# Reading modulation and weight blocks in 128-row transfers, and running V's first products chunk by chunk

## The chip, the cores and the metric

The kernel runs on one core of a Trainium2 chip. The metric is the device time of one execution in microseconds; of several runs the median is given.

## The reference

One transformer block over 2048 tokens of width D = 448 with 16 heads of 28, all in fp32. A condition vector `c` (448 values) gives six rows of modulation:

```python
mod = (silu(c) @ w_mod).reshape(1, 6, 1, 448)      # w_mod: 448 x 2688
sa, ca, ga, sb, cb, gb = (mod[:, i] for i in range(6))
h = layernorm(x) * (1 + ca) + sa
x = x + ga * mha(h, wqkv, wo)                      # softmax attention, wqkv: 448 x 1344
h = layernorm(x) * (1 + cb) + sb
x = x + gb * gmlp(h, w_in, w_sp, b_sp, w_out)      # GELU, spatial mix over 2048 tokens
```

The change concerns the start: `sa` and `ca`, the first layer norm, and V's products of the first 512 tokens.

## The kernel before

**Staging.** The program is one long order written by hand: each engine runs its instructions in the order of the text, and waits come only from data and buffers. Tokens are taken in four groups of 512 (`g`), each of four tiles of 128 (`t`, `kt`). The width of 448 is cut into four chunks `c` of 128, 128, 128 and 64 rows; the chunks are worked in the order 0, 2, 1, 3. Products keep fp32 accuracy by two parts: `hi` is the value rounded for the fast fp32 matmul, `lo` the remainder. The operand `hT[g]` has seven blocks: 0 to 2 the `hi` and 3 to 5 the `lo` of chunks 0 to 2, block 6 `hi` and `lo` of the 64-row chunk one above the other. A weight has eight: 0 to 2, 3 to 5 likewise, 6 the `hi` of the 64-row block on both halves of the partitions, 7 its `lo` with zeros. A product is eleven steps `(a, b)` (a block of `hT`, a block of the weight) that add up in one bank: `STEPS`.

**The 64-row block (the z block).** `load_z` (L86 to L88) reads the last 64 rows of a weight twice, into partitions 0 to 63 and 64 to 127, with two DMAs. It is used for V's weight and for parts `a` (512 columns) and `b` (384 columns) of the q/k weight (`load_w`, L194), and later for `wo` (`wo_load`), and the two halves of `w_in` (`win_first`, tile `wraw`; `win_load`, tile `raw_in`).

**Modulation.** `w_mod` comes as four blocks of 112 rows for each of three pairs (`load_mod`, L176). For pair 0 (`sa`, `ca`) all four blocks are scaled by `silu(c)` and added up over rows on ScalarE and VectorE (L380, L241, `mod_last` L407); `mod_dot` (L420) sums over partitions with a product by ones, so that each chunk's columns lie on partitions; `mod_cols` (L427, L429) puts them into `cols["ca"]` and `cols["sa"]`. Pairs 1 and 2 are added up later in the same way (`mod_acc`).

**First group.** `load_x(0)` is issued from the ScalarE and SyncE queues. `pe_fill` (L230) runs products on TensorE whose result is not used, between the real ones. `ln_stat`, `ln_rs`, `ln_norm` (L279 to L298) normalise x, `xn` gets a copy of its last 64 columns on ScalarE, and `tp_first` (L371) transposes it into four banks `tps[c]`. `h_hi(c)` (L441, ScalarE) scales and rounds a chunk into `hT[0]`; `h_full(c)` (L436, VectorE) gives it unrounded, `h_lo(c)` (helper L84) the remainder. `wv_hi` (L352, L354) and `wv_lo` (L84) split V's weight. `v_step(j, kts)` (L477) runs step `j` for the given tiles.

**After V.** ScalarE runs `qk_hi(0)`, `qk_hi(2)`, `qk_hi(3)` (L512, the `hi` of part `a`), `v_copy` of tile 0 (L309), `qk_hi(1)`, and `v_copy` of the others; VectorE runs the statistics of group 1, `qk_lo` for blocks 0, 2, 1, 3, and `ln_norm(1)`. TensorE goes on with `qk_unit((0, 3), 0, order=HI_FIRST)` (L323), two banks at a time: steps (0,0), (2,2), (3,0), (5,2), (1,1), (4,1), (6,6), and then the `lo` steps. Step (1,1) is the first that reads what `qk_hi(1)` writes, so it is the ninth product. Then come the transposes of group 1 (L117), and so on through four groups, the attention, the output product and the MLP.

**DMA.** SyncE issues nearly all transfers, in the order of the text; an issue waits until the buffer is free and an earlier transfer on the same semaphore has landed. In the attention `n_bcast` (L707) reads a row per 512 queries with `[:, None, :].broadcast_to([4, 32, 512])` into 128 partitions.

Of the kernel before, what the change touches and what calls it, by code (L numbers as in the profile page):

```python
# [33 lines left out]
def tile_adaln_mha_gmlp(ctx, tc, x, wqkv, wo, w_in, w_spT, b_sp, w_out, cT, w_mod, out):  # L34
# [21 lines left out]
    silu = const.tile([112, 4], F32, name="silu")  # L56
# [6 lines left out]
    heapF = dpool.tile([128, 4 * 896], F32R, name="heapF", tag="heapF")  # L63
# [17 lines left out]
    wqk = Halves(4, hview(heapD[2], 0, 4, 896), hview(heapF, 0, 4, 896))  # L81

# [3 lines left out]
    def load_z(eng, dst, src):  # L86
        eng.dma_start(dst[0:64], src)
        eng.dma_start(dst[64:128], src)  # L88
# [71 lines left out]
    ones_r = e2.tile([112, 128], F32R, name="ones_r")  # L160
# [6 lines left out]
    def bank(name):  # L167
        k = mode[0](name) if mode[0] else banks[0]
        banks.remove(k)
        banks.append(k)  # L170
        return ring.tile([128, 512], F32, name=name, tag=f"b{k}")

    def load_mod(pair, eng):
        for k in range(4):
            wms[pair, k] = e1.tile([112, 2, D], F32, name="wm", tag=("wm", "wm", "raw")[pair], bufs=4)
            eng.dma_start(wms[pair, k], w_mod[:, pair, k])  # L176

    def load_x(g, eng):
        xg = e1.tile([128, 4, D], F32, name="xg")
        for t0, t1 in ((0, 1), (1, 2), (2, 4)) if g == 0 else ((0, 4),):  # L180
            (act if t1 - t0 == 1 else eng).dma_start(xg[:, t0:t1, :], x[g, :, t0:t1])
        for t in range(4):
            xts[4 * g + t] = xg[:, t, :]
# [23 lines left out]
    cc_t = e1.tile([112, 4], F32, name="cc_t", bufs=1)  # L207
# [7 lines left out]
    pool.memset(wqk[64:128, 7, 0:896].bitcast(F32), 0.0)  # L215
# [3 lines left out]
    ec = e1.tile([112, 4], F32, name="ec", bufs=1)  # L219
    act.activation(ec, cc_t, AF.Exp, scale=-1.0)  # L220
    dve.tensor_scalar(out=ec, in0=ec, scalar1=1.0, scalar2=None, op0=ALU.add)
    dve.reciprocal(ec, ec)
    dve.tensor_tensor(out=silu, in0=cc_t, in1=ec, op=ALU.mult)

    pcs = {c: bank("pc") for c in (0, 2)}
# [8 lines left out]
    def mod_acc(pair, k):  # L234
        if k == 0:
            accs[pair] = e2.tile([112, 2, D], F32, name="acc")
        wm, acc = wms.pop((pair, k)), accs[pair]
        if k == 0:
            dve.tensor_scalar(out=acc, in0=wm, scalar1=silu[:, 0:1], scalar2=None, op0=ALU.mult)
        else:  # L240
            dve.scalar_tensor_tensor(out=acc, in0=wm, scalar=silu[:, k : k + 1], in1=acc, op0=ALU.mult, op1=ALU.add)  # L241

    def mod_split(pair, eng, pool_l, tag_l, bufs_l):

        acc = accs.pop(pair)
        accs[pair] = []
        for part in range(2):
            h = stage.tile([128, 512], F32R, name="acc_h", tag="qf")[0:112, :D]
            l = pool_l.tile([112, D], F32R, name="acc_l", tag=tag_l, bufs=bufs_l)
# [32 lines left out]
    def ln_rs(g, a, e):  # L282
        mv, rs = mv1[g]
        rstd_of(mv[:, a:e, 1], rs[:, a:e], e - a)
# [15 lines left out]

    def v_mm(kt):
# [47 lines left out]
    def wv_hi(i):  # L349
        h = wv[:, i if i < 3 else 6, :]  # L350
        if i == 2:
            pool.tensor_copy(h, raws["v", i])  # L352
        else:
            act.activation(h, raws["v", i], AF.Copy)  # L354
# [8 lines left out]


    tps, fs = {}, {}
# [3 lines left out]
    def tp_first(t):  # L369
        for c in range(4):  # L370
            pe.transpose(tps[c][:, t * 128 : (t + 1) * 128], xn1[0][t][:, c * 128 : (c + 1) * 128], ident)  # L371

    x0, x3 = xts[0], xts[3]
    pe_fill(14, x0)
    ln_stat(0, (0, 1))
    ln_rs(0, 0, 2)
    ln_stat(0, (2, 3))
    ln_rs(0, 2, 4)
    accs[0] = e2.tile([112, 2, D], F32, name="acc")
    act.activation(accs[0], wms.pop((0, 0)), AF.Copy, scale=silu[:, 0:1])  # L380
    ln_norm(0, (0, 1))
    mod_acc(0, 1)
    tp_first(0)
    tp_first(1)
    ln_norm(0, (2, 3))
    mod_acc(0, 2)
    pe_fill(5, x3)
    tp_first(2)
    tp_first(3)
    pe_fill(2, x3)  # L390

    acc0 = [stage.tile([128, 512], F32, name="acc0", tag="qh")[0:112] for _ in range(2)]
    wm3 = wms.pop((0, 3))

    def mod_last(c):
        for part in (1, 0):
            if c < 3:
                o = acc0[part][:, c * 128 : (c + 1) * 128]  # L400
                a, w = (v[:, part, c * 128 : (c + 1) * 128] for v in (accs[0], wm3))
            else:
                o = acc0[part][:, 384:512].rearrange("p (r n) -> p r n", n=64)
                a, w = (
                    v[:, part, 384:D].rearrange("p (r n) -> p r n", r=1).broadcast_to([112, 2, 64]) for v in (accs[0], wm3)
                )
            dve.scalar_tensor_tensor(out=o, in0=w, scalar=silu[:, 3:4], in1=a, op0=ALU.mult, op1=ALU.add)  # L407

    def mod_dot(c, which):
        if c == 1:  # L410
            pcs[c] = ps_o.tile([128, 512], F32, name="pc", tag="o")
        if c == 3:
            pcs[c] = pcs[1][:, 2:4]
        for i, part in enumerate((1, 0)):
            cs = slice(c * 128, (c + 1) * 128)
            if which == "C":
                o, lhs, rhs = 2 + i, wm3[:, part, cs], silu[:, 3:4]
            else:
                o, lhs, rhs = i, (accs[0][:, part] if which == "A" else acc0[part])[:, cs], ones[:112, 0:1]
            pe.matmul(pcs[c][:, o : o + 1], lhs, rhs, start=True, stop=True)  # L420

    def mod_cols(c):
        for i, (nm, plus1) in enumerate((("ca", 1.0), ("sa", 0.0))):
            o = cols[nm][:, c : c + 1]
            if c == 0:
                a, b = pcs[c][:, i : i + 1], pcs[c][:, 2 + i : 3 + i]
                dve.tensor_scalar(out=o, in0=a, scalar1=b, scalar2=plus1, op0=ALU.add, op1=ALU.add)  # L427
            else:
                dve.tensor_scalar(out=o, in0=pcs[c][:, i : i + 1], scalar1=plus1, scalar2=None, op0=ALU.add)  # L429

    def h_full(c):
        if c < 2:
            fs[c] = e1.tile([128, 512], F32, name="hfull")
        else:
            fs[c] = stage.tile([128, 512], F32, name="hfull", tag="qf")
        dve.tensor_scalar(  # L436
            out=fs[c], in0=tps[c], scalar1=cols["ca"][:, c : c + 1], scalar2=cols["sa"][:, c : c + 1], op0=ALU.mult, op1=ALU.add
        )
# [12 lines left out]
    for i in (0, 2, 1, 3):  # L451
        load_w("a", i, sp)
    wv_hi(0)
    wv_hi(2)
    mod_dot(0, "C")
    mod_dot(0, "A")
    mod_last(2)
    pe_fill(2, x3)
    mod_dot(2, "all")
    pe_fill(4, x3)  # L460
    mod_cols(0)
    h_hi(0)
    mod_cols(2)
    h_hi(2)
    mod_last(1)
    mod_last(3)
    wv_hi(1)
    wv_lo(0, dve)


    order = [STEPS[j] for j in (0, 1, 6, 2, 3, 4, 7, 5, 8, 9, 10)]
    pvs = [(kt, bank("pv") if kt < 3 else None) for kt in range(4)]
# [9 lines left out]
    mod_dot(1, "all")  # L482
    mod_cols(1)
    h_hi(1)
    wv_hi(3)
    v_step(1, (0, 1, 2))
    mod_dot(3, "all")
    wv_lo(2, dve)
    h_full(0)
    mod_cols(3)  # L490
    h_hi(3)
    v_step(2, (0, 1, 2))
    pvs[3] = (3, ps_o.tile([128, 512], F32, name="pv", tag="o"))
    for j in range(3):
        v_step(j, (3,))
    h_lo(0, pool)
    h_full(2)
    h_full(1)
    wv_lo(1, dve)
    h_lo(2, dve)  # L500
    h_lo(1, dve)
    h_full(3)
    h_lo(3, dve)
    wv_lo(3, dve)
    load_x(2, sp)
    for i in (0, 2, 1, 3):
        load_w("b", i, sp)
    for j in range(3, NST):
        v_step(j, range(4))

# [976 lines left out]
```

## Time and profile before

| | us |
|---|---|
| median of 3 runs | 1397.21 |
| lowest, highest | 1396.95, 1399.44 |
| span of the profiled execution, first to last instruction | 1394.0 |
| TensorE busy in it | 1386.8 |
| VectorE, ScalarE, GpSimd busy | 1027.5, 776.5, 285.5 |

For the profiled execution the profile has the span alone, without what lies around it; the median of the runs lies 3.2 us above that span. Lines of the profile give a start and a duration in us, the engine (PE is TensorE's products, PEld its weight loads, DVE VectorE, ACT ScalarE, POOL GpSimd, SPq SyncE's issue of DMAs), the line of the kernel, the tiles written and read, the shape, and in brackets the idle time before, with what ended it. A product in plain fp32 appears as two passes.

### The profile page before, as it was taken

The page shows a single profiled execution, that of the slowest core. Times are in us where ns is not written, and L with a number is a line of the kernel's source. Part 1 is how long each engine was busy: PE and PEld are TensorE (multiplying, and loading weights), DVE is VectorE, ACT ScalarE, POOL GpSimd, SP SyncE. Part 2 cuts the span into 40 slices and gives each one's busy share as a digit, 9 for nine tenths or more (in the row PEclk, how much of TensorE's full clock was granted, in tenths as well). Part 3 has the DMA queues.
Part 4 walks back from the last instruction along what each step waited for, and adds up shares of the span by engine and source line. Part 5 has one row for each costly group of instructions (what it writes and reads, how often), then busy time and mean ns, then how long its engine had stood idle before and what let it go on. Part 6 is the DMA issues. An engine that isn't in the chain of part 4 may idle for free.

```text
span 1394.0 us, 20327 instructions
## 1 busy us (share of the span) xinstructions
PE 1386.8 (99%) x7180; PEld 988.9 (71%) x7180; DVE 1027.5 (74%) x1741; ACT 776.5 (56%) x1490; POOL 285.5 (20%) x306
## 2 busy tenths in 40 slices
PE   8999999999999999999999999999999999999999
PEld 8888655555555555555555555988998888888888
DVE  7798888888888888888888851750366655668574
ACT  4623677777766667777777779363234544434211
POOL 2234213221224143323200021000142330000000
PEclk9999999999999999999999999999999999999999
DMA  8564644565465556554323002434103333445453
GB/s 265 150 178 177 196 109 151 172 177 154 149 178 167 162 159 189 165 161 150 111 68 76 21 18 73 161 123 140 46 4 110 113 109 112 143 137 163 142 174 110
DMA packets 99377, 187.01 MB, mean 134 GB/s; under 512 B 17736, under 2 KB 29130, under 8 KB 96730
## 3 DMA queue, kind: packets, MB, share of 16 engines
q1 hardware_dynamic: 96558, 181.42, 42.6%
q10 hardware_dynamic: 2718, 4.30, 0.9%
q8 instruction: 56, 0.92, 0.3%
q14 instruction: 45, 0.37, 0.1%
HBM read 130.42 MB, written 50.46 MB: 130 GB/s over the span
## 4 chain that ended last, share of the span: by engine, by line
PE 99%; DMA 0%; DVE 0%; ACT 0%; ACTq 0%; issue 0%
PE st_ps L666 19%; PE o_ps L681 17%; PE mt L634 17%; PE acc L1250 7%; PE acc L1252 7%; PE acc L1251 7%; PE z_ps L1176 5%; PE pq L323 5%; PE z_ps L1062 5%; PE wo_ps L928 3%; PE pv L305 2%; PE y_ps L1357 2%; PE y_ps L1358 2%; PE y_ps L1356 2%; PE tp L117 1%; PE pv L477 1%
## 5 line engine op out<-in xcount | busy, mean ns | idle before, releaser
L639 DVE TENSOR_REDUCE pm<-mt 128x1 f32<-128x512 f32 x1024 | 631.1, 682 | 85.6 <-PE mt L634 85.5
L670 ACT ACTIVATE P<-st_ps 128x512 f32<-128x512 f32 x1024 | 514.5, 628 | 200.8 <-PE st_ps L666 200.7
L666 PE MATMUL st_ps<-qst,kst 128*128 128x512 f32 x1024 | 404.1, 406 | 0.0
L634 PE MATMUL mt<-kst,qst 128*128 128x512 f32 x1024 | 401.7, 392 | 0.0
L666 PEld LDWEIGHTS st_ps<-qst,kst 128*128 128x128 f32 x1024 | 191.2, 187 | 141.2 <-issue 93.1
L681 PE MATMUL o_ps<-P,V 128*32 128x512 f32 x2048 | 247.1, 598 | 0.0
L634 PEld LDWEIGHTS mt<-kst,qst 128*128 128x128 f32 x1024 | 192.4, 188 | 31.8
L791 POOL TENSOR_TENSOR ws_raw<-ws_raw 128x512 f32<-128x512 f32 x80 | 103.2, 1290 | 293.8 <-DMA ws_raw<-in_w_spT_dram 290.9
L1138 ACT ACTIVATE wsp_h<-raw_sp 128x512 fp32r<-128x512 f32 x112 | 70.0, 630 | 153.6 <-PE acc L1252 102.9
L84 DVE TENSOR_TENSOR wsp_l<-raw_sp,wsp_h 128x512 fp32r<-128x512 f32 x112 | 80.7, 730 | 83.1 <-ACT wsp_h L1138 82.3
L681 PEld LDWEIGHTS o_ps<-P,V 128*32 128x32 f32 x2048 | 54.7, 109 | 122.0 <-issue 114.0
L1250 PE MATMUL acc<-wsp_h,heapA 128*128 128x512 f32 x224 | 87.3, 390 | 0.0
L1251 PE MATMUL acc<-wsp_l,heapA 128*128 128x512 f32 x224 | 87.2, 389 | 0.0
L1252 PE MATMUL acc<-wsp_h,heapA 128*128 128x512 f32 x224 | 87.2, 389 | 0.0
L1251 PE MATMUL acc<-wsp_l,heapB 128*128 128x512 f32 x174 | 67.7, 389 | 0.0
L1252 PE MATMUL acc<-wsp_h,heapB 128*128 128x512 f32 x174 | 67.7, 389 | 0.0
L1250 PE MATMUL acc<-wsp_h,heapB 128*128 128x512 f32 x174 | 67.7, 389 | 0.0
L323 PE MATMUL pq<-heapD,heapD 128*128 128x512 f32 x196 | 61.8, 390 | 0.0
L1180 DVE BATCH_NORM_STATS2 stz<-z 128x6 f32<-128x448 f32 x32 | 19.9, 625 | 50.4 <-ACT z L1179 30.1
L1250 PEld LDWEIGHTS acc<-wsp_h,heapA 128*128 128x128 f32 x224 | 42.0, 188 | 8.9 <-DVE cD L1256 0.3
L1252 PEld LDWEIGHTS acc<-wsp_h,heapA 128*128 128x128 f32 x224 | 42.0, 188 | 8.8
L1251 PEld LDWEIGHTS acc<-wsp_l,heapA 128*128 128x128 f32 x224 | 42.0, 188 | 8.6
(222 smaller groups left out, 1597.0 us busy)
## 6 DMA issues: line engine op xcount, KB each, us to landing
ws_raw<-in_w_spT_dram SPq DMA_DIRECT2D x160, 256.0 KB
ws_scr<-ws_raw SPq DMA_DIRECT2D x80, 256.0 KB
raw_sp<-ws_scr SPq DMA_DIRECT2D x80, 256.0 KB
kst<-qk_scr SPq DMA_DIRECT2D x45, 224.0 KB
qst<-qk_scr SPq DMA_DIRECT2D x45, 224.0 KB
raw_sp<-in_w_spT_dram SPq DMA_DIRECT2D x32, 256.0 KB
qk_scr<-qh SPq DMA_DIRECT2D x28, 256.0 KB
qk_scr<-ql SPq DMA_DIRECT2D x28, 256.0 KB
```

Of the source, the lines that this page charges most:

```text
L84: eng.tensor_tensor(out=dst, in0=a, in1=hi.bitcast(F32), op=ALU.subtract)
L323: pe.matmul(pq, wqk[:, b, m * 128 : (m + 1) * 128], hT[g][:, a, :], start=j == 0, stop=j == NST - 1)
L634: pe.matmul(mt, qst[h % 3][:, t * 128 : (t + 1) * 128], kst[h % 3][:, kb * 512 : (kb + 1) * 512], start=True, stop=True)
L639: dve.tensor_reduce(out=pms[h][:, t, kb : kb + 1], in_=mt, axis=AX.X, op=ALU.max)
L666: pe.matmul(st, kst[h % 3][:, kt * 128 : (kt + 1) * 128], qst[h % 3][:, qb * 512 : (qb + 1) * 512], start=True, stop=True)
L670: act.activation(p, st, AF.Exp, scale=SCALE)
L681: pe.matmul(otile[h][32 * qb : 32 * qb + 32, :], V[:, kt, h, :], ptiles.pop((u, qb)), start=kt == 0, stop=kt == NT - 1)
L791: pool.tensor_tensor(out=a, in0=a, in1=b, op=SUMS[i // 16][2])
L1138: act.activation(hi, raw, AF.Copy)
L1250: pe.matmul(acc[i], zh, hi, start=st == 0, stop=False)
L1251: pe.matmul(acc[i], zh, lo, start=False, stop=False)
L1252: pe.matmul(acc[i], zl, hi, start=False, stop=st == 7)
```

## The change

- **w_mod, pair 0**: laid out by column chunk, each chunk one transfer of 128 rows (`load_mod0`): for a chunk of n columns, three row blocks of 128 for both parts, and the last 64 rows of the two parts one above the other. `silu` gets five columns to match. Pairs 1 and 2 are read by blocks of 128 rows, the last 64 rows of both parts in one block.
- **Order of the loads**: w_mod and V's weight alternate by chunk; x of the first group comes in four transfers; part `a` of the q/k weight is issued further down in the text, after V's last weight step.
- **z blocks**: `load_z` is one DMA with a source of `[2, 64, n]`, the 2 repeated.
- **Modulation**: chunk 0 goes straight through TensorE (`mod_direct`, eight products into one column each); the other chunks are scaled and added up by chunk (`acc_first` on ScalarE, `acc_rest` on VectorE), then `mod_dot` and `mod_cols`.
- **V**: the eleven steps are ordered by chunk, so that chunk 0's three steps run before chunk 2's data are made, and so on. `h_full` moves to ScalarE, `h_lo(0)` to VectorE, `wv_hi(2)` to ScalarE. The fills between the transposes and the dots go, 13 remain at the start.
- **Buffers**: pair 0 of w_mod lies in the buffer that later holds half of the q/k weight; the memset of its block 7 moves behind V.

```diff
     def load_z(eng, dst, src):
-        eng.dma_start(dst[0:64], src)
-        eng.dma_start(dst[64:128], src)
+        eng.dma_start(dst, src[None, :, :].broadcast_to([2, 64, src.shape[-1]]))
...
+    def load_mod0(c, eng):
+        n = 128 if c < 3 else 64
+        v = wm0[:, c * 896 : c * 896 + 7 * n]
+        eng.dma_start(v, w_mod0[c * 896 * 128 : (c * 896 + 7 * n) * 128].rearrange("(r n) -> r n", r=128))
+        wms[0, c] = v[:, 0 : 6 * n].rearrange("r (k p n) -> r k p n", k=3, p=2), v[:, 6 * n :]
...
-    load_mod(0, sp)
     for i in (0, 2, 1, 3):
+        load_mod0(i, sp)
         load_w("v", i, sp)
     load_x(1, sp)
...
+    def half_rows(wm, outs):
+        for part, o in enumerate(outs):
+            dve.scalar_tensor_tensor(out=o, in0=wm, scalar=silu[:, 3 + part : 4 + part], in1=o, op0=ALU.mult, op1=ALU.add)
...
+    def mod_direct(c):
+        wm, wh = wms.pop((0, c))
+        for i, part in enumerate((1, 0)):
+            for k in range(3):
+                pe.matmul(pc_of(c, i), wm[:, k, part, :], silu[:, k : k + 1], start=k == 0, stop=False)
+            pe.matmul(pc_of(c, i), wh, silu[:, 3 + part : 4 + part], start=False, stop=True)
+
+    def acc_first(c):
+        n = 128 if c < 3 else 64
+        o = acc0[c] = stage.tile([128, 512], F32, name="acc0", tag="qh")[:, 0 : 2 * n].rearrange("p (a n) -> p a n", n=n)
+        act.activation(o, wms[0, c][0][:, 0], AF.Copy, scale=silu[:, 0:1])
+
+    def acc_rest(c):
+        (wm, wh), o = wms.pop((0, c)), acc0[c]
+        for k in (1, 2):
+            dve.scalar_tensor_tensor(out=o, in0=wm[:, k], scalar=silu[:, k : k + 1], in1=o, op0=ALU.mult, op1=ALU.add)
+        half_rows(wh, [o[:, part] for part in range(2)])
...
+    x0 = xts[0]
+    pe_fill(13, x0)
+    ln_norm(0, (0, 1))
     wv_hi(0)
+    mod_direct(0)
+    for t in (0, 1):
+        for c in range(4):
+            tp_first(c, (t,))
+    acc_first(2)
+    ln_norm(0, (2, 3))
+    for c in (0, 2, 1, 3):
+        tp_first(c, (2, 3))
     mod_cols(0)
+    acc_rest(2)
     h_hi(0)
+    h_full(0)
     wv_lo(0, dve)
+    order = [(0, 0), (0, 3), (3, 0), (2, 2), (2, 5), (5, 2), (1, 1), (1, 4), (4, 1), (6, 6), (6, 7)]
...
     v_step(0, (0, 1, 2))
+    mod_dot(2)
+    mod_cols(2)
+    h_lo(0, dve)
+    acc_first(1)
+    wv_hi(2)
     v_step(1, (0, 1, 2))
+    v_step(2, (0, 1, 2))
+    h_hi(2)
+    h_full(2)
+    acc_rest(1)
     wv_lo(2, dve)
+    mode[0] = lambda name: tp0_bank
+    pvs.append((3, bank("pv")))
+    mode[0] = None
     for j in range(3):
         v_step(j, (3,))
+    v_step(3, range(4))
+    mod_dot(1)
+    mod_cols(1)
+    wv_hi(1)
+    h_hi(1)
     h_full(1)
+    acc_first(3)
+    h_lo(2, dve)
     wv_lo(1, dve)
+    v_step(4, range(4))
+    v_step(5, range(4))
     h_lo(1, dve)
+    acc_rest(3)
+    v_step(6, range(4))
+    mod_dot(3)
+    mod_cols(3)
+    wv_hi(3)
+    h_hi(3)
     h_full(3)
     h_lo(3, dve)
     wv_lo(3, dve)
+    for i in (0, 2, 1, 3):
+        load_w("a", i, sp)
     load_x(2, sp)
     for i in (0, 2, 1, 3):
         load_w("b", i, sp)
-    for j in range(3, NST):
+    for j in range(7, NST):
         v_step(j, range(4))
```

More of the change, by code (lines that the diff above doesn't have):

```diff
@@ L33, in tile_adaln_mha_gmlp @@
 @with_exitstack
[L34 removed]
+def tile_adaln_mha_gmlp(ctx, tc, x, wqkv, wo, w_in, w_spT, b_sp, w_out, cT, w_mod0, w_mod, out):
     nc = tc.nc
@@ L55, in tile_adaln_mha_gmlp @@
     dve.memset(mhalf, -0.5)
-    silu = const.tile([112, 4], F32, name="silu")
+    silu = const.tile([128, 5], F32, name="silu")
     cols = {}
@@ L214, in tile_adaln_mha_gmlp @@
     pool.memset(wv[64:128, 7, :].bitcast(F32), 0.0)
-    pool.memset(wqk[64:128, 7, 0:896].bitcast(F32), 0.0)
     pool.memset(V[:, :, :, DH:32], 1.0)
[L219 to L225, printed above, removed]
+    ec = e1.tile([128, 5], F32, name="ec", bufs=1)
     wu = bank("wu")
@@ L299, in ln_norm @@
             xn1.setdefault(g, []).append(xn)
+    ln_stat(0, (0, 1))
+    act.activation(ec, cc_t, AF.Exp, scale=-1.0)
+    dve.tensor_scalar(out=ec, in0=ec, scalar1=1.0, scalar2=None, op0=ALU.add)
+    dve.reciprocal(ec, ec)
+    dve.tensor_tensor(out=silu, in0=cc_t, in1=ec, op=ALU.mult)
+    ln_rs(0, 0, 2)
+    ln_stat(0, (2, 3))
+    ln_rs(0, 2, 4)
     def v_mm(kt):
@@ L361, in wv_lo, with tp_first @@
             sub(eng, wv[0:64, 7, :], raw[0:64], wv[0:64, 6, :])
-    tps, fs = {}, {}
+    tps, fs, acc0 = {}, {}, {}
+    tp0_bank = banks[0]
     for c in (0, 2, 1, 3):
         tps[c] = bank("tp")
-    def tp_first(t):
-        for c in range(4):
+    def tp_first(c, ts):
+        for t in ts:
             pe.transpose(tps[c][:, t * 128 : (t + 1) * 128], xn1[0][t][:, c * 128 : (c + 1) * 128], ident)
[L373 to L413, printed above, removed]
-        for i, part in enumerate((1, 0)):
[L415 to L420, printed above, removed]
+    def pc_of(c, i):
+        return wu[:, 256 + 2 * c + i : 257 + 2 * c + i]
@@ new lines, in acc_rest, with mod_dot @@
+    def acc_rest(c):
[3 more added lines that the diff above has]
+        half_rows(wh, [o[:, part] for part in range(2)])
+    def mod_dot(c):
+        for i, part in enumerate((1, 0)):
+            a = acc0[c][:, part]
+            for r0, r1 in ((0, 128),) if c < 3 else ((0, 64), (64, 128)):
+                pe.matmul(pc_of(c, i)[r0:r1], a, ones[:, 0:1], start=True, stop=True)
@@ L449, in h_lo @@
             sub(eng, hT[0][64:128, 6, :], fs[3][64:128], hT[0][64:128, 6, :])
-    for i in (0, 2, 1, 3):
-        load_w("a", i, sp)
+    x0 = xts[0]
+    pe_fill(13, x0)
+    ln_norm(0, (0, 1))
     wv_hi(0)
[L454 to L460, printed above, removed]
+    mod_direct(0)
[6 more added lines that the diff above has]
+        tp_first(c, (2, 3))
     mod_cols(0)
+    acc_rest(2)
     h_hi(0)
[L463 to L467, printed above, removed]
+    h_full(0)
     wv_lo(0, dve)
-    order = [STEPS[j] for j in (0, 1, 6, 2, 3, 4, 7, 5, 8, 9, 10)]
-    pvs = [(kt, bank("pv") if kt < 3 else None) for kt in range(4)]
+    order = [(0, 0), (0, 3), (3, 0), (2, 2), (2, 5), (5, 2), (1, 1), (1, 4), (4, 1), (6, 6), (6, 7)]
+    pvs = [(kt, bank("pv")) for kt in range(2)]
+    pvs.append((2, ps_o.tile([128, 512], F32, name="pv", tag="o")))
     def v_step(j, kts):
@@ L507, in tile_adaln_mha_gmlp @@
         load_w("b", i, sp)
-    for j in range(3, NST):
+    for j in range(7, NST):
         v_step(j, range(4))
+    heapF = dpool.tile([128, 4 * 896], F32R, name="heapF", tag="heapF")
+    wqk = Halves(4, hview(heapD[2], 0, 4, 896), hview(heapF, 0, 4, 896))
+    pool.memset(wqk[64:128, 7, 0:896].bitcast(F32), 0.0)
     def qk_hi(i):
@@ L1471 @@
         "w_out": inputs["B_w_out"],
-        "cT": inputs["c"].reshape(4, 112).T,
-        "w_mod": _np.asarray(inputs["w_mod"]).reshape(4, 112, 3, 2, 448).transpose(1, 2, 0, 3, 4),
+        "cT": cT,
+        "w_mod0": _np.concatenate([rows(0, c, min(c + 128, 448)) for c in (0, 128, 256, 384)]),
+        "w_mod": _np.concatenate([_np.concatenate([blocks(i, k) for k in range(4)]) for i in (1, 2)]),
     }
```

69 lines of the change are left out of this document (30 added, 39 removed).

## The prediction

> **What bounds the kernel now.** First the page: its span, and its chain that ended last.
>
> ```profile
> span 1394.0 us, 20327 instructions
> PE 99%; DMA 0%; DVE 0%; ACT 0%; ACTq 0%; issue 0%
> ```
>
> TensorE sets the end almost everywhere, so a microsecond by which its unbroken stream starts sooner or later is a microsecond of the result. The change touches the first 25 us. So the second view is the chain of waits in order of time over the first stages (start, duration, what):
>
> ```profile
> 16.20 0.16 DVE col_sa L429
> 16.39 0.79 ACT heapD L441
> 17.22 8.02 PE pv L477 x38
> 25.24 5.02 PE pq L323 x22
> 30.25 1.75 PE tp L117 x16
> ```
>
> The last wait outside TensorE is the ScalarE step at 16.39 (`h_hi(1)`). From 17.22 on, V's remaining 38 products (0.211 each), the first q/k unit (22 products, 0.228 each) and the next transposes (0.109 each) follow without a gap. The reference point of the sum is the **ninth q/k product**, the first that needs `qk_hi(1)`: 25.24 + 8 x 0.228 = 27.07 us. Its shift in the changed kernel is the shift of the end.
>
> **Prices.** Timeline (start, duration, engine, line, tiles), with the waits in brackets:
>
> ```profile
> 3.61 5.06 PE L230 MATMUL wu<-ones,xg 128*128 128x128 f32 x28 [3.61 <-DMA xg<-in_x_dram]
> 12.30 0.51 PE L420 MATMUL pc<-silu,wm 112*128 112x1 f32 x4
> 14.90 0.85 PE L477 MATMUL pv<-wv,heapD 128*128 128x448 f32 x3
> 13.74 1.54 ACT L441 ACTIVATE heapD<-tp,col_sa,col_ca 128x512 fp32r<-128x512 f32 x2 [0.84 <-DVE col_sa L427]
> 14.32 1.13 DVE L407 SCALAR_TENSOR_TENSOR acc<-wm,silu,acc 112x128 f32<-112x128 f32 x4
> 19.62 1.29 DVE L84 TENSOR_TENSOR heapD<-hfull,heapD 128x512 fp32r<-128x512 f32 x2
> 18.51 1.15 ACT L512 ACTIVATE heapD<-raw 128x512 fp32r<-128x512 f32 x2
> 21.41 0.63 ACT L512 ACTIVATE heapF<-raw 128x512 fp32r<-128x512 f32 x1 [1.76 <-DMA raw<-in_wqkv_dram]
> 24.67 0.55 ACT L309 ACTIVATE V<-pv 128x448 f32<-128x448 f32 x1 [2.62 <-PE pv L477]
> 25.11 0.62 ACT L512 ACTIVATE heapD<-raw 128x512 fp32r<-128x512 f32 x1
> ```
>
> The reader should see the ScalarE order at the end: `qk_hi(0)`, `qk_hi(2)`, then `qk_hi(3)`, which waited until 21.41 for the z block of part a, then `v_copy(0)`, then `qk_hi(1)` at 25.11. Today that wait ends 3.3 us before `v_copy(0)` could start, so it costs nothing.
>
> Next the windows of the transfers (columns: stretch, length, busy of PE, PEld, DVE, ACT, POOL, clock, DMA share of 16 engines, GB/s), and the two ends of the one kind of transfer here that has a leading broadcast, `n_bcast` (source `[4, 32, 512]`, the 32 repeated, 256 KB):
>
> ```profile
> 2.00:4.00 2.00, 0.39 (x2) 0.42 (x3) 0.52 (x4) 1.15 (x2) 1.56 (x2) 1.00 0.94 324
> 4.00:6.00 2.00, 2.00 (x11) 2.00 (x11) 1.05 (x4) 0.00 (x0) 0.00 (x0) 1.00 1.07 354
> 6.00:12.00 6.00, 5.93 (x47) 5.55 (x47) 5.44 (x12) 1.85 (x5) 2.19 (x4) 1.00 1.03 288
> 16.00:18.00 2.00, 1.93 (x12) 1.71 (x13) 1.87 (x7) 1.41 (x3) 0.31 (x1) 1.00 1.03 385
> 213.40:214.60 1.20, 1.20 (x7) 0.98 (x6) 1.20 (x3) 1.20 (x4) 1.19 (x1) 1.00 0.25 99
> 210.79 0.58 SPq L707 DMA_DIRECT2D rb<-r_scr  x1
> 217.04 1.28 POOL L710 TENSOR_TENSOR osb<-osb,rb 128x512 f32<-128x512 f32 x1 [2.33 <-DMA rb<-r_scr]
> 838.07 0.59 SPq L707 DMA_DIRECT2D rb<-r_scr  x1
> 842.96 1.28 POOL L710 TENSOR_TENSOR osb<-osb,rb 128x512 f32<-128x512 f32 x1 [9.93 <-DMA rb<-r_scr]
> ```
>
> **Part 1, w_mod in 128 rows, by chunk.** The loads of 112 rows ran in 6 to 12 us at 288 GB/s; in 16 to 18, where whole 128-row blocks were on the way, 385. To the last w_mod chunk the changed queue carries x (0.92 MB), w_mod (1.61) and three V blocks (0.69): 3.21 MB. From 2.0 us, where the share jumps to 0.94, that ends at 10.3 at 385 GB/s and at 13.1 at 288. I take 10.6, near the 128-row rate, since all of these are now 128 rows. The first chunk is due when the fills end (8.2, below) and lies at 5.6 to 6.8 in the stream, so its landing has over 1 us of cover; the later chunks have more.
>
> **Part 2, V's products chunk by chunk.** The fills are 26 passes instead of 28. Two windows of the fill line (stretch, length, busy PE and PEld, clock, DMA share, GB/s) give their pitch:
>
> ```profile
> 3.60:7.00 3.40, 3.39 (x16) 3.40 (x17) 1.00 1.05 342
> 7.20:8.50 1.30, 1.30 (x13) 1.28 (x12) 1.00 1.01 276
> ```
>
> Sixteen passes took 3.4 us (0.21 each), then 0.11 each. So the fills end at 3.61 + 17 x 0.21 + 9 x 0.11 = 8.2. `mod_direct(0)` is 8 products of two passes; four passes took 0.51 alone, some 0.11 each in a row: 1.7, to 9.9. Then transposes: chunk 0 is whole after 10 of 16, with the drain at 11.2. `h_hi(0)` 0.79: 12.0. V's first product starts there, against 14.90 before, but the waits now lie inside V:
> - three products 0.63, `mod_dot(2)` and its two columns 0.7 (0.51 with the drain, 0.16 and a hand-over): 13.3. VectorE's `h_lo(0)` 0.65: 13.95. Ten products (steps 1 and 2 are partly there already, tile 3's three, and step 3) 2.1: 16.05.
> - `mod_dot(1)` and its columns 0.7: 16.75. `h_hi(1)`, `h_full(1)`, both now on ScalarE, 1.54: 18.3. VectorE: `h_lo(1)` 0.65, then `acc_rest(3)` (two of 128 elements at 0.28, two of half that, about 0.2): 1.0, to 19.95.
> - `mod_dot(3)`, four products of half width, and columns 0.85; `h_hi(3)` and `h_full(3)` 1.54; `h_lo(3)` 0.65: 23.0. The last eight products 1.7: **24.7**.
>
> TensorE's own work would fill only up to 22.6 (12.0, 44 products, 1.3 of dots); DVE and ACT hold it. With 0.1 more in each of a dozen hand-overs it is 26.0. V thus ends 0.5 us earlier (2.6 earlier to 0.8 later). The fills taken out between are worth nothing: TensorE waits there anyway. `h_lo(0)` and `wv_hi(2)` leave POOL, whose steps were not on the chain; the wqk memset now waits for w_mod's last reader (20 us), still before `qk_hi(3)`.
>
> **Part 3, z blocks in one transfer.** `load_z` becomes one DMA whose source is `[2, 64, n]` with the 2 repeated. No such transfer is in the trace; the nearest is `n_bcast`. While it ran alone (213.40 to 214.60) a quarter of the 16 engines was busy and moved 99 GB/s: four engines, one for each entry of the outermost dimension, 24.7 GB/s each. So I take two engines for the outermost 2. The price for one engine's 64 KB was, less the issue, 842.96 - 838.66 = 4.30 us in the quiet case, 217.04 - 211.37 = 5.67 beside other loads. 2.66 of it is the transfer at 24.7 GB/s, 1.64 lies around it; in the busy case the transfer took 4.03. For V's z block (112 KB an engine) that makes 4.7 to 7.1 us, for part a's (128 KB) 5.3 to 8.1, where sixteen engines need 0.6 and 0.7.
>
> The Trainium skill speaks against this form: "DMA: Bandwidth & Descriptors", section "Rules for kernel authors", says that an outermost dimension under 16, a leading zero-stride broadcast for one, confines the whole DMA to at most that many engines. The quarter in the trace agrees for 4; no run here shows 2 yet. By that rule the sum is the one that follows; with sixteen engines it would be that of the first rival.
>
> That both z blocks and the rest share the two engines in order of issue is my inference. Then they carry: the stream to 10.6; V's z, 6.6 (fourteen engines are busy with x(1) and part a, so near the slow end) to 17.2; their sixteenth of x(1) (57 KB) 2.35; of three blocks of a (49 KB) 2.0; a's z, 5.9 (the others have little left by then, so near the quick end) to 27.45; landing 0.8, half of the 1.64: **28.25**. Then `qk_hi(3)` 0.53, `v_copy(0)` 0.44, both by start-to-start in the rows above, `qk_hi(1)` 0.62, hand-overs 0.06: the ninth q/k product at 29.9 instead of 27.07, **+2.85 us**. TensorE has done its eight by 26.5 and waits. Behind `qk_hi(3)` on ScalarE stand the V copies and `xn`'s pads; behind `qk_hi(1)` VectorE's `qk_lo(1)`, `qk_lo(3)` and `ln_norm`, which shift with it and so give nothing back. V's own z block lands at 18.0 and is wanted by `wv_hi(3)` before `h_hi(3)` at 20.8: covered by 2 us.
>
> Bounds: with everything at the free rate a's z lands at 10.3 + 4.7 + 2.35 + 2.0 + 5.3 + 0.8 = 25.4, and the shift is 0.0; with the slow ends 13.1 + 7.1 + 2.35 + 2.0 + 8.1 + 0.8 = 33.4, +8.0.
>
> The part-a loads move down in the text, but on SP they still follow x(1) and no longer wait for w_mod's buffers. The three later z loads are hidden:
>
> ```profile
> 556.57 0.60 SPq L88 DMA_DIRECT2D wo_raw<-in_wo_dram  x1
> 562.56 1.16 POOL L750 TENSOR_TENSOR wo_raw<-wo_raw,bc_ga 128x448 f32<-128x448 f32 x1
> 783.35 0.59 SPq L88 DMA_DIRECT2D wraw<-in_w_in_dram  x1
> L1006 ACT ACTIVATE heapA<-wraw x4: 935/936/937, 866.0 to 868.5; 128x896 fp32r<-128x896 f32 x4
> 944.40 0.59 SPq L88 DMA_DIRECT2D raw_in<-in_w_in_dram  x1
> 959.24 0.94 ACT L95 ACTIVATE heapF<-raw_in 128x896 fp32r<-128x896 f32 x1
> ```
>
> (The fourth row is the line's summary: count, shortest, median and longest in ns, first and last start.) The first has 6 us, the second 80, the third 15 (224 KB an engine: 9.3 to 14.1). If the cover is gone, POOL or ACT starts a few us late, with TensorE banks in hand. The two halves of w_mod's last block in the later pairs cost VectorE a fraction of a us under TensorE's products.
>
> **The sum.** +2.85 on a span of 1394.0; the median of the runs shown, 1397.21, lies 3.2 above that span, and I add the shift to it: **1400.1**. The 0.2% that a measurement of this kernel can tell from no change is 2.8 us.
>
> **Rivals.**
> - *The broadcast is spread over sixteen engines, or the two blocks use different ones* (faster, no wait): a's z lands before 22, `qk_hi(3)` follows at once, and V's 0.5 us gain stands: 1396.7. It decides if a's z lands before 24.9. Against it speaks the quarter above. Chance 0.12.
> - *Two engines at the free rate*: shift 0.0, 1397.2. For it: 99 GB/s held on four engines; against it the 4.03 beside other loads. Chance 0.14.
> - *The stall cools TensorE*: it waits from 26.5 to 29.9, 3.4 us, and the fills show a slow first 3.4 us after idleness. If the pitch doubles again for as long, 3.4 us do the work of 1.7: +4.55, 1401.8. Against it: nothing in this trace shows a restart after a short wait. Chance 0.18. The skill's "TensorE: Matmul & The Clock Gate", Part 1, gives an idle window of about 3.4 us for this; the first fills agree with its busy window.
> - *DVE and ACT overlap better than I sum, and no z wait*: V ends at 22.6, 1394.6. Chance 0.03.
>
> **The numbers.** Forecast (two engines, contended) 0.53, over +1 to +6. Half of it and a bit (0.31) lies above 2.8 us, with the cooled case 0.49 slower. Faster by over 0.2% needs a little more than the last rival gives: 0.03. The rest, 0.48, is within. The range runs from the no-wait case, 1396.3, to 1403.3 (+6.1), the slow end of a's z leaving out its most extreme sum.
>
> **What would show it.** Right: `qk_hi(3)` (heapF from raw) starts near 28 with a long DMA wait; the DMA share falls to an eighth while a z block runs alone; V starts at about 12 and ends near 24.7 with gaps before `mod_dot(3)`; the ninth q/k product near 30. Wrong: a's z lands before 25, a gap over 3 us remains inside V, or SP's order puts the z blocks elsewhere.

## The result, and the profile after

| | before | after |
|---|---|---|
| median, us | 1397.14 (9 runs) | 1400.67 (9 runs) |
| lowest, highest | 1395.40, 1399.44 | 1399.50, 1402.07 |
| span of the profiled execution | 1394.0 | 1399.8 |

The ratio is 1.0029, with a 95% interval of 1.0019 to 1.0038: slower by 3.5 us. The forecast was 1400.1. The two profiled executions lie 5.8 us apart, since one is at the low end of its runs and the other in the upper half of its own. So steps are compared by place below, and kernels by medians.

The page of the changed kernel, its span and the engines' shares of the chain that ended last, reads nearly as before:

```profile
span 1399.8 us, 20294 instructions
PE 98%; DMA 1%; issue 0%; SPq 0%; ACT 0%; DVE 0%
```

One per cent more stands on transfers. Below, "the z wait" is the wait for the z block of part `a`: through `qk_hi(3)`, `v_copy(0)` and `qk_hi(1)` on ScalarE it holds TensorE's ninth q/k product. The chain of waits, over the stretch that the prediction showed (start, duration, what):

```profile
11.95 11.14 DMA raw<-in_wqkv_dram
23.09 1.05 ACT heapD L512 x2
24.14 3.94 issue
28.07 0.63 ACT heapF L512
28.70 0.43 ACT V L324
29.14 0.53 ACT heapD L512
29.71 5.08 PE pq L338 x14
34.79 1.75 PE tp L114 x16
```

The unbroken stream of TensorE now begins at the ninth q/k product, 29.71. It was 27.07 by the prediction's reckoning of before. ScalarE's `qk_hi(3)` (heapF, L512) starts at 28.07. The time ahead of it is named "issue", that is, no releaser was found for it. The windows tell what it was (columns as in the prediction):

```profile
25.00:26.00 1.00, 1.00 (x6) 0.91 (x5) 0.93 (x5) 0.00 (x0) 0.00 (x0) 1.00 0.13 51
26.00:28.00 2.00, 1.59 (x7) 0.96 (x6) 1.62 (x5) 0.00 (x0) 0.35 (x2) 1.00 0.13 52
30.50:33.90 3.40, 3.40 (x9) 2.62 (x8) 2.17 (x5) 1.48 (x6) 0.00 (x0) 0.50 0.95 290
```

Up to 28 an eighth of the sixteen DMA engines is at work and moves 51 to 52 GB/s, while ScalarE stands still: part `a`'s z block on two engines. The third row shows what followed the wait. From 30.5 to 33.9 the granted clock is 0.50, and nine products were started where fifteen fit at the full clock. The fourteen products from 29.71 took 5.08 us, where 14 x 0.228 = 3.2 was due. The transposes of group 1 start at 34.79 against 30.25, so the stream is 4.5 us late. After that the offset hardly moves: it lies between +4.4 and +4.9 up to 1340 us. In the last 50 us it grows by another 0.9, to +5.5 at the last product: from 1350 to 1380 the trace has 147 products where the kernel before has 149, at a clock of 1.00 in both. The profiles of v_two, z_one and early_bc (below) show these slower products too, with 146 or 147; those of x_bc, x_old and z_two, with 150, do not. What causes them was not tried.

TensorE's timeline around V:

```profile
12.43 0.87 PE L457 MATMUL pv<-wv,heapD 128*128 128x448 f32 x3 [0.21 <-ACT heapD L422]
20.94 0.40 PE L408 MATMUL wu<-ones,acc 128*64 128x1 f32 x8 [0.94 <-DVE acc L247]
23.87 1.89 PE L457 MATMUL pv<-wv,heapD 128*128 128x448 f32 x8 [0.70 <-DVE heapD L82]
25.60 1.99 PE L338 MATMUL pq<-heapD,heapD 128*128 128x512 f32 x8
29.71 1.41 PE L338 MATMUL pq<-heapD,heapD 128*128 128x512 f32 x4 [2.12 <-ACT heapD L512]
```

V starts 2.5 us earlier than before and ends a little later: the first q/k product starts at 25.60, against 25.24. The last row shows TensorE's wait of 2.12 us.

### The profile page after: what moved, and what is told of

Same layout as the page of the kernel before. It is cut to its first block, busy times and chain, and to the rows that moved or that the text cites. A ratio compares the mean times of both kernels' runs of the same rounds, so it can differ in the third digit from the quotient of the medians.

```text
span 1399.8 us, 20294 instructions
## 1 busy us (share of the span) xinstructions
PE 1387.9 (99%) x7164; PEld 987.4 (71%) x7164; DVE 1025.6 (73%) x1744; ACT 779.5 (56%) x1497; POOL 283.6 (20%) x304
## 4 chain that ended last, share of the span: by engine, by line
PE 98%; DMA 1%; issue 0%; SPq 0%; ACT 0%; DVE 0%
PE st_ps L666 18%; PE o_ps L681 17%; PE mt L634 17%; PE acc L1250 6%; PE acc L1252 6%; PE acc L1251 6%; PE z_ps L1176 5%; PE pq L338 5%; PE z_ps L1062 5%; PE wo_ps L928 3%; PE pv L320 2%; PE y_ps L1357 2%; PE y_ps L1356 2%; PE y_ps L1358 2%; PE tp L114 1%; DMA raw<-in_wqkv_dram 1%
```

## The experiments

My theory was that part `a`'s z block on two engines sets the loss. The rivals were V's end and the VectorE work behind it, the clock, and the way x is loaded. Each time below stands beside the runs of the kernel before on the same chip; "over" is the difference of the two medians.

| kernel | V's order | z blocks | first x | over, us | ratio, 95% |
|---|---|---|---|---|---|
| the change | changed | broadcast | four | +3.5 | 1.0029 [1.0019, 1.0038] |
| z_two | changed | two transfers | four | +2.4 | 1.0016 [1.0007, 1.0025] |
| x_bc | changed | broadcast | three | +1.6 | 1.0011 [1.0002, 1.0020] |
| x_old | changed | two transfers | three | +1.3 | 1.0012 [1.0003, 1.0021] |
| early_bc | chunk 3 moved up | broadcast | four | +5.6 | 1.0037 [1.0024, 1.0049] |
| early_two | chunk 3 moved up | two transfers | four | -1.2 | 0.9988 [0.9979, 0.9997] |
| z_one | as before | broadcast | three | +6.7 | 1.0048 [1.0036, 1.0061] |
| a_two | changed | V's by broadcast, a's by two transfers | four | +2.5 | 1.0018 [1.0009, 1.0027] |
| v_two | changed | V's by two transfers, a's by broadcast | four | +2.6 | 1.0017 [1.0008, 1.0027] |
| early3 | chunk 3 moved up | one transfer of 128 rows | four | -1.0 | 0.9994 [0.9985, 1.0003] |
| early3_x | chunk 3 moved up | one transfer of 128 rows | three | -1.3 | 0.9993 [0.9984, 1.0002] |
| fill_wait | changed | broadcast | four | +2.7 | 1.0024 [1.0015, 1.0033] |

The intervals are about 0.1% wide to either side, some 1.3 us, so differences of about 1 us between two rows are hints only.

**z_two: the broadcast taken out.**

```diff
     def load_z(eng, dst, src):
-        eng.dma_start(dst, src[None, :, :].broadcast_to([2, 64, src.shape[-1]]))
+        eng.dma_start(dst[0:64], src)
+        eng.dma_start(dst[64:128], src)
```

> The changed kernel with the z blocks read by two DMAs of 64 rows each, as before; all else as changed. Theory (the broadcast confines each z block to two engines, and part a's z block is late): a's z lands before 22 us, qk_hi(3) follows qk_hi(2) at once, TensorE is not held at the ninth q/k product, which starts at V's end plus eight products, 25.6 + 1.8 = 27.4 us against 27.07 in the kernel before; the clock stays at 1.00; the time is that of the kernel before plus 0.4 us (0.0 to +1.0), some 3 us under the changed kernel. Rival (the new layout of w_mod or the chunk order is what costs): the ninth product stays near 29.7 us and the time near +3.5 us.

Measured: 1398.96 against 1396.58. Most of the loss is still there, so taking the z wait away does not take the loss away, although it stood on the chain. TensorE's timeline of this kernel:

```profile
9.47 0.80 PE L391 MATMUL wu<-silu,wm 128*128 128x1 f32 x6 [0.63 <-DMA wm<-in_w_mod_dram]
11.25 3.46 PE L382 MATMUL tp<-ident,xn 128*128 128x128 f32 x16
14.35 0.90 PE L458 MATMUL pv<-wv,heapD 128*128 128x448 f32 x2
```

Here the first w_mod chunk was waited for, and the sixteen transposes took 3.46 us. They took 1.94 in the changed kernel: this run was at half clock from 11.48 to 14.89. Four of the eleven runs have a lower granted clock (0.998 or 0.999); the seven at 1.000 have a median of 1398.79, still 2.2 over, so the half clock is not what makes up the +2.4.

**z_one: the broadcast alone, in the kernel before.**

```diff
     def load_z(eng, dst, src):
-        eng.dma_start(dst[0:64], src)
-        eng.dma_start(dst[64:128], src)
+        eng.dma_start(dst, src[None, :, :].broadcast_to([2, 64, src.shape[-1]]))
```

> The kernel before with one edit: the z blocks read by one DMA with the leading broadcast of 2. Theory: V's z block takes two engines for 5.5 to 7 us behind a stream that ends near 14.4, a's z another 5.5 to 7 behind the two engines' share of x(1) and part a; a's z lands at 29 to 31, the ninth q/k product starts at 30.7 to 32.7 instead of 27.07, TensorE is idle long enough for a spell of half clock, and the time is 4 to 8 us over the kernel before, more than the changed kernel. Rival (the broadcast is harmless, or costs only issue time): within 0.5 us of the kernel before.

Measured: 1403.32 against 1396.58, +6.7. ScalarE's timeline, and the window behind the wait:

```profile
29.39 0.63 ACT L511 ACTIVATE heapF<-raw 128x512 fp32r<-128x512 f32 x1 [6.04 <-DMA raw<-in_wqkv_dram]
```

```profile
31.90:35.20 3.30, 3.30 (x9) 2.57 (x8) 2.09 (x5) 1.40 (x5) 0.00 (x0) 0.50 1.05 268
```

`qk_hi(3)` waits 6.04 us for its block, here named in the row, and half clock follows. The same edit costs 6.7 us here and about 1.2 us in the changed kernel (after against z_two): something in the changed kernel lies over it.

**a_two and v_two: one z block by two transfers, the other by the broadcast.** a_two splits part `a`'s, v_two V's.

```diff
-            load_z(eng, raw, wqkv[384:448, c0 : c0 + n])
+            src = wqkv[384:448, c0 : c0 + n]
+            if kind == "a":
+                eng.dma_start(raw[0:64], src)
+                eng.dma_start(raw[64:128], src)
+            else:
+                load_z(eng, raw, src)
```

> The changed kernel with part a's z block read by two DMAs of 64 rows; V's and all later z blocks keep the broadcast. Theory (the two blocks add up in the queue of the same two engines, and V's alone is covered): V's z lands at 18, a's z within 1 us after the last other block of part a, near 22.5; no wait at the ninth product (27.4 us), time +0.4 us (0 to +1.2) over the kernel before. Rival (each block costs its share by itself): about half of the changed kernel's +3.5.

> The changed kernel with V's z block read by two DMAs of 64 rows; part a's and all later z blocks keep the broadcast. Theory (the two blocks add up in the queue of the same two engines): V's z lands before 14, a's z 6 us after the other blocks of part a, at 21 to 24, while qk_hi(3) could start at 24.2; no wait at the ninth product (27.4 us), time +0.4 us (0 to +1.2) over the kernel before. Rival (a's z is late by itself, 28 us as in the changed kernel): +2.5 to +4.5.

Measured: 1399.04 and 1399.16, +2.5 and +2.6, both the same as z_two and both over the 0.4 that was expected; v_two's time even lies in its rival's range. The traces decide: in neither kernel is there a wait at the ninth product. So one block on two engines costs nothing that these medians tell, and the wait needs the two in a row. Here is v_two's chain of waits:

```profile
24.70 0.63 ACT heapF L517
28.43 1.88 DVE heapF L82 x3
30.31 1.71 DVE xn L301 x4
32.06 1.64 PE tp L114 x13
```

Part `a`'s block, alone, landed just before 24.70; ScalarE waited 0.47 us for it, and TensorE not at all. The transposes now wait for `xn`, that is for VectorE: four statistics, four `qk_lo`, then `ln_norm(1)`, all behind the last V work. Offsets of matching products against the kernel before are +0.62 at the first q/k product and +1.69 at the end of these transposes. This 1.07 us is what the z wait had covered.

**x_old: z_two, with x loaded as before.**

```diff
-        for t0, t1 in ((0, 1), (1, 2), (2, 3), (3, 4)) if g == 0 else ((0, 4),):
-            (act if t1 == 1 else eng).dma_start(xg[:, t0:t1, :], x[g, :, t0:t1])
+        for t0, t1 in ((0, 1), (1, 2), (2, 4)) if g == 0 else ((0, 4),):
+            (act if t1 - t0 == 1 else eng).dma_start(xg[:, t0:t1, :], x[g, :, t0:t1])
```

> The kernel of run z_two (changed kernel, z blocks by two DMAs) with one more edit undone: x of the first group comes as before, two single tiles from the ScalarE queue and the other two in one transfer from SyncE's, instead of one and three. Theory (in the changed kernel the single-tile transfers on one queue starve the DMA engines between 3.5 and 5.5 us, 143 to 204 GB/s against 378 to 407 before, so x's last tile and w_mod's first chunk land 1 to 2 us late, TensorE idles after its fills and its clock may halve): the rate in 4 to 5 us is back near 400, the first chunk lands by 7.5, TensorE goes from the fills into mod_direct without a wait, no spell of half clock before 30 us, and the time is 0.5 to 1.5 us under z_two, which leaves +1 to +1.9 us over the kernel before (V's end and VectorE's work on group 1). Rival (the start does not matter, V is held by ACT and DVE alone): same as z_two, +2.4.

Measured: 1398.08 against 1396.83, +1.3. The same stretch of the windows, from the kernel before, the changed one and x_old in turn:

```profile
4.00:5.00 1.00, 1.00 (x6) 1.00 (x6) 0.77 (x3) 0.00 (x0) 0.00 (x0) 1.00 1.07 407
```

```profile
4.00:5.00 1.00, 1.00 (x6) 1.00 (x7) 0.96 (x3) 0.00 (x0) 0.00 (x0) 1.00 0.82 204
```

```profile
4.00:5.00 1.00, 1.00 (x7) 1.00 (x6) 0.21 (x2) 0.00 (x0) 0.00 (x0) 1.00 1.05 332
```

With single-tile transfers the engines are not filled (0.82) and move half the bytes; in z_two, which differs from x_old in x alone, it was 0.73 and 143 GB/s. Its worth in time is 1.1 us by medians beside z_two, but the two intervals overlap.

**early3 and early3_x: chunk 3 moved up.** The z blocks come in one transfer of 128 rows from an input in which the 64 rows stand twice (early3_x also loads x as before). One of group 1's four statistics also moves ahead of V's last steps (the later `ln_stat` call, not shown, has one less).

```diff
     acc_rest(1)
     wv_lo(2, dve)
+    wv_hi(1)
+    acc_first(3)
+    acc_rest(3)
...
-    wv_hi(1)
     h_hi(1)
     h_full(1)
-    acc_first(3)
     h_lo(2, dve)
     wv_lo(1, dve)
     v_step(4, range(4))
-    v_step(5, range(4))
-    h_lo(1, dve)
-    acc_rest(3)
-    v_step(6, range(4))
     mod_dot(3)
     mod_cols(3)
     wv_hi(3)
     h_hi(3)
     h_full(3)
+    v_step(5, range(4))
+    h_lo(1, dve)
+    ln_stat(1, (0,))
+    v_step(6, range(4))
     h_lo(3, dve)
```

> The changed kernel with three edits: the z blocks of V and parts a and b come from a doubled 128-row array in one contiguous transfer each; chunk 3's modulation sums run right after chunk 1's, and its dot after the fifth V step, instead of after the seventh; one of group 1's four statistics runs before VectorE's last two V steps. Theory (the rest of the loss is VectorE's and ScalarE's chain: chunk 3's columns wait for h_lo(1) and the sums, then h_hi(3), h_full(3), h_lo(3) follow one by one, and behind them group 1's statistics and normalisation): V ends near 23.6 to 24.2 instead of 25.7, the transposes of group 1 start at 28.9 to 30.0 instead of 32 to 33, and the time is 1.5 to 2.8 us under z_two, about that of the kernel before (-0.8 to +0.9). Rival (the rest of the loss is the start alone): within 0.5 us of z_two, +2 to +2.9.

> Run early3 with the x transfers of run x_old as well. Theory (both account for the rest): transposes of group 1 near 28.5 to 29.5 us against 30.25 before, full clock throughout, time 0.5 to 2 us under the kernel before. Rival (the two shares overlap): as the better of the two, near the kernel before.

Measured: 1395.85 and 1395.56 against 1396.83. Neither is told apart from the kernel before, but both are well below z_two. How x is loaded makes no difference here (0.3 us). The chain of early3:

```profile
18.73 5.32 PE pv L457 x24
24.04 4.99 PE pq L338 x22
29.03 1.75 PE tp L114 x16
```

The gap before chunk 3's column sums is gone, and from 18.73 on nothing but TensorE stands on the chain.

**fill_wait: the change, with TensorE kept at work during its wait.** Nine products whose result is not used stand between the eighth and the ninth q/k product.

```diff
+            if j == 4:
+                for _ in range(fills):
+                    pe.matmul(fb[:, 0:128], ident, ones, start=True, stop=True)
...
-    qk_unit((0, 3), 0, order=HI_FIRST)
+    qk_unit((0, 3), 0, order=HI_FIRST, fills=9)
```

> The changed kernel with nine products without use (18 passes, about 2.0 us) between the eighth and the ninth product of the first q/k unit, where TensorE waits for qk_hi(1); they write to a bank that is free then. Theory (the idle time there halves TensorE's clock for 3.4 us in about half of the runs, which costs 1.9 us more): no spell of half clock after 25 us, the ninth product starts at 29.6 to 30.0 as in the changed kernel, the group 1 transposes follow 2.6 to 3.0 us later than before instead of 4.5, and the runs lie together at +2.0 to +3.0 us. Rival (the spell has another cause, such as the waits inside V): spells stay, +3.5 us or, with the fills on the way, more.

Measured: 1399.52 against 1396.83, +2.7. Its chain:

```profile
28.32 2.01 PE fb L341 x18
30.33 3.28 PE pq L343 x14
33.61 1.75 PE tp L114 x16
```

The fourteen products behind the wait take 3.28 us instead of 5.08, so the half clock was the idleness's doing. The transposes still start 3.4 us late, not 2.6 to 3.0 as expected: V ended later in this run (the first q/k product starts at 26.35), and the fills may hold the ninth product by 0.2, since `qk_hi(1)` was done at 30.09. The nine runs of the changed kernel are in two groups, 1399.5 to 1400.4 with a granted clock of 1.000 and 1400.7 to 1402.1 with 0.998 or 0.999. Of the eleven runs here nine lie within 0.9 us of each other.

**early_bc and early_two: the order of early3, with the z blocks by the broadcast and by two transfers.** early_bc is early3's edit of the order alone on the changed kernel; early_two adds z_two's.

> The changed kernel with chunk 3's column sums and one tile of group 1's statistics moved ahead in V's order (as in early3), but with both z blocks read by the broadcast. Theory (the z wait and V's late end lie over each other, so the later one alone is paid): V ends near 24.1, the ninth q/k product still starts at 29 to 29.7 when part a's z block has landed, and the time stays at 1399.5 to 1401, the idle time before that product growing from 2.1 us to over 3. Rival (the terms add up): the 2.2 us that the order was worth without the broadcast come off here too, 1398.2 to 1398.8.

> As early_bc, but each z block read by two plain transfers as before the change. Theory (the order of V was the other loss, and how the z block is read matters only as long as it keeps off the two-engine queue): 1395.5 to 1396.6, with V's end at 24.0 to 24.6 and no wait for part a's z block. Rival (early3 was quick because its z block came in one contiguous transfer of 128 rows): the time is that of z_two or x_old, 1398 to 1399.

Measured: 1402.84 and 1396.08 against 1397.27. The two differ in the broadcast alone, and by 6.8 us, as z_one does from the kernel before (6.7). TensorE's timeline and the window behind the wait, early_bc:

```profile
24.37 2.00 PE L338 MATMUL pq<-heapD,heapD 128*128 128x512 f32 x8
30.68 1.53 PE L338 MATMUL pq<-heapD,heapD 128*128 128x512 f32 x4 [4.32 <-ACT heapD L513]
```

```profile
31.40:34.70 3.30, 3.30 (x10) 2.55 (x9) 2.25 (x5) 1.56 (x6) 0.00 (x0) 0.50 1.01 346
```

V ends 1.2 us earlier than in the changed kernel, TensorE waits 2.2 us longer (the z block also came later, and was used from 29.05), and the kernel's loss is 2.0 us larger. All five of its runs had a granted clock of 0.997 to 0.999, so the half clock came each time. The theory's first half held (the earlier V end is worth nothing with the broadcast) and its number did not: 1402.84 instead of 1401 at most. It left out the clock and the later landing. early_two's chain:

```profile
18.46 5.30 PE pv L458 x24
23.77 5.01 PE pq L339 x22
28.78 1.75 PE tp L115 x16
```

These steps are 1.47 us earlier than in the kernel before, of which 0.95 is left at the last product. The time is 1.2 us lower, with an interval that ends just below 1. It is as quick as early3, so the contiguous 128-row source was not needed. It is the only version here whose interval lies below the kernel before.

**x_bc: the change, with x loaded as before** (the diff of x_old).

> The changed kernel with the first group's x in three transfers as before, two tiles in the last. Theory (single-tile transfers delay the first w_mod chunk, but part a's z block sets the end of this stretch): 355 GB/s or more in 4 to 5 us instead of 204, the first w_mod chunk at or before the end of the fills, and the time at most 0.6 lower, 1400.0 to 1400.7. Rival (the start is a term of its own): about 0.9 lower, 1399.5 to 1399.9. Second rival (it does nothing, since transposes and column sums wait for each other anyway): 1400.7.

Measured: 1398.86 against 1397.27, 1.9 us less over than the change, more than any of the theories gave. The issue of part `a`'s z block (SyncE), first in the changed kernel and then in x_bc, and x_bc's wait on TensorE:

```profile
11.95 0.54 SPq L85 DMA_DIRECT2D raw<-in_wqkv_dram  x1
```

```profile
10.55 0.53 SPq L85 DMA_DIRECT2D raw<-in_wqkv_dram  x1
28.80 1.21 PE L338 MATMUL pq<-heapD,heapD 128*128 128x512 f32 x4 [0.60 <-ACT heapD L512]
```

The stream ahead of the z block goes faster, so it is issued 1.4 us and used 0.9 us earlier. The idle time falls to 0.60, and the half clock stays away (one run of eleven has 0.999). Against x_old, which differs in the broadcast alone, it is 0.3 us over: with x loaded as before, the cost of the broadcast on top of the late V is not told from nothing. So x's part in the change's loss lies at the end of the queue, in the landing of the z block, more than at its beginning.

## Why the prediction was right or wrong

**Time.** 1400.67 lies 0.6 above the forecast and inside the range; it is slower by 3.5 us. The sum had one term, the z wait's 2.85, and that measured 2.64. The rest is the cooled clock: 1.9 us in about half of the runs, some 0.9 on the average (an estimate from the profile and the runs' clocks), 3.5 together; fill_wait, without the half clock, was at +2.7. The errors below did not show in the time, because the z wait lay over them: that the total came out so near is in part luck. The lower end of the range, 1396.3, is called the no-wait case there, but the first rival puts that case at 1396.7; the bound had no sum of its own.

**Two engines for the leading 2: right.** The DMA share of 0.13 at 51 to 52 GB/s is two engines at 25 to 26 GB/s each, where `n_bcast` gave 24.7. The page "DMA: Bandwidth & Descriptors" of the Trainium skill, section "Rules for kernel authors", says that such an outermost dimension confines a transfer to at most that many engines; this trace agrees for 2. The block's landing is recorded at 28.00 (forecast 28.25), `qk_hi(3)` started at 28.07, the ninth q/k product at 29.71 (29.9), a shift of 2.64 (2.85). That the two blocks queue up on the same engines, which was an inference, is shown by a_two and v_two. The first two rivals (no wait) are refuted by the same rows. The terms on the way were less good: the last w_mod chunk landed at 13.4, not 10.6 (288 GB/s, the slow end, had given 13.1), and yet V's z block landed at 18.12 (18.0). It runs beside that stream rather than after it, and the two errors cancelled, which was luck.

**The cooled clock: this rival happened too.** I gave it 0.18 because it wanted 3.4 us of waiting. The profiled run had a wait of 2.12 and then 3.4 us at half clock, and about half of the runs show it in their clock. The offset grows by 1.9 us there, 4.53 against 2.64, near the 1.7 that I had worked out for it. The failed step is the condition, not the price. The Trainium skill's "TensorE: Matmul & The Clock Gate", Part 1, gives a window of 3413 ns that runs freely and says that the clock falls after at least one idle window. The length of the slow stretch agrees (30.51 to 33.92); the condition doesn't, since the changed kernel's profile has no wait so long, and 2.12 us was enough. Waits of 4.05 (z_one) and 4.32 us (early_bc) brought it in every run, 0.60 (x_bc) did not in its profile. The length of the wait is not all: in z_two a half-clock stretch followed a wait of 0.63 us soon after the start. What decides it in the other runs was not tried.

**V's end: wrong, by a sum too short.** Forecast 24.7, 0.5 earlier than before; the first q/k product started at 25.60, 0.4 later. V's first product came at 12.43 (12.0), the columns of chunk 1 were done at 17.45 (16.75), chunk 3's column sums waited for `acc_rest(3)`, which ran 19.64 to 20.88 (1.24 instead of 1.0, and 0.9 later than summed), and the last eight products started at 23.87 (23.0). The term for `acc_rest(3)` was 0.24 too small, and the rest came as a tenth or a few at each hand-over. My own upper bound of 26.0, with 0.1 more for each, was nearer than the value that I took.

**"Shift with it and so give nothing back": wrong.** I treated `qk_lo` and `ln_norm(1)` as work that hangs on the z wait. It hangs on the end of V as well: without the z wait VectorE's chain holds group 1's transposes 1.07 us longer than V's end alone would (v_two; x_old from +0.33 to +1.39 likewise). This wait was missed altogether, and so was what it means: V's end with its VectorE tail and the z wait lie over each other. By medians the broadcast costs 1.2 us on top of the late V (0.3 with x as before; neither is clear of the noise) and 6.8 on top of the early one. The late order (chunk 3 and the one statistic) costs 3.6 us without the broadcast, and with it the late kernel is even the quicker by 2.0.

**"Over 1 us of cover" for the first w_mod chunk: wrong.** It assumed the stream of before, and overlooked that x in four transfers has single tiles only. It landed at 8.36 in the changed kernel and at 9.33 in z_two, where it was waited for; the fills end at 8.26 and 8.85. Beside this the start varies by itself. These are the fills of the changed kernel and of x_bc, the same 26 passes:

```profile
3.75 4.51 PE L228 MATMUL wu<-ones,xg 128*128 128x128 f32 x26 [3.75 <-DMA xg<-in_x_dram]
```

```profile
3.66 5.67 PE L228 MATMUL wu<-ones,xg 128*128 128x128 f32 x26 [3.66 <-DMA xg<-in_x_dram]
```

1.2 us lie between them, with no wait in either: the full clock comes sooner or later (its first record is at 6.62 in one trace and at 8.96 in the other). The sum took this as one fixed 3.4 us.

**The later z loads** were called hidden. From the transposes of group 1 to 1340 us the offset stays within 0.4 of +4.5, so they cost that at most; none was tried by itself. The 0.9 us of the last stage is not theirs: x_bc has the same loads and does not show it.

**What stays open.** How much of z_two's +2.4 is x at the start is not settled: its runs at full clock still have a median 2.2 over the kernel before, but its interval and that of x_old's +1.3 overlap. Why early_bc's z block came 1 us later than the change's, though issued at nearly the same time, was not tried.

## What to carry to other kernels

Two late arrivals before the same point cover each other: removing one shows only what sticks out, and the second then sets the time. Before an early start is booked as a gain, follow every engine up to the next point where TensorE needs it, and try each loss with the other one gone. Where a wait on TensorE can't be avoided, half clock may follow it (here in about half of the runs after 2 us, in all after 4); and a transfer with a short leading dimension is no cheap form of two, above all where a second one is queued behind it.

## What the runs showed of the hardware

An issue can be held up by what was queued before it. SyncE's issue of the next x, a plain transfer, behind the two z blocks in the changed kernel:

```profile
12.74 6.14 SPq L185 DMA_DIRECT2D xg<-in_x_dram  x1
```

It took 6.14 us, where the same line took 0.54 in the kernel before, and whatever stood behind it on that queue came later. The issue of this x took 4.02 to 7.22 us in the five kernels in which two broadcast blocks stood ahead of it, and 0.82 at most in a_two and v_two with one, and 0.54 at most in the others. Second, 2.12 us of idleness on TensorE can be followed by 3.4 us at half clock, in some runs of a kernel and not in others. Third, x as single tiles from one queue left the DMA engines partly idle (share 0.82, 204 GB/s against 407 in the kernel before; 0.73 and 143 in z_two against 1.05 and 332 in x_old, which differ in that alone).
